# A new order of all units in a hand-scheduled attention and maxout FFN kernel

## The chip, the core and the metric

The kernel runs on one core of one Trainium2 chip. The metric is the device time of one execution in microseconds. Every engine of the core (PE for matmuls and transposes, DVE, ACT and POOL for elementwise work, SP for the DMA queue) takes its own instructions in the order in which the program gives them, and waits for the others by semaphores.

## What is computed

For 4 batches of 768 tokens with 8 heads of 64, attention with a window of 96 tokens back and 8 global tokens, and a distance bias per head; then an FFN whose hidden layer is the largest of three projections:

```python
scores = scale * np.matmul(q, k.transpose(0, 1, 3, 2))
keep = is_global | is_local            # first 8 tokens, or 0 <= row - col < 96
scores = np.where(keep, scores - slopes * dist, -1e9)
a = softmax(scores)
x = np.matmul(a, v)                    # (B, H, S, D) -> (3072, 512)
h = np.maximum(np.maximum(x @ w1, x @ w2), x @ w3)   # 512 -> 768
out = h @ w_out                                       # 768 -> 512
```

Inputs and output are float32; the matmuls work on bf16 casts.

## The kernel before, in words

The tokens are cut into 24 tiles of 128, T = 0 to 23, six to a batch. With a window of 96 a tile needs only its own keys and those of the tile before it, plus the 8 global keys, which are copied over the first 8 columns of the tile before, out of the window's reach. For the FFN the tiles are gathered in seven chunks of 4, 2, 2, 4, 4, 4, 4 (sizes, L89).

The whole order of work is the string SCHEDULE (L25). It is read from left to right (L475); each word is a unit, a letter with numbers, and each unit appends its instructions to the queues of its engines, the DMAs among them to SP's. A word thus stands ahead of a later one only on the engines that both use. A last number (`how`) often picks the engine: 0 ACT, 1 DVE, 2 POOL (`copies`, L176), 4 a DMA transpose for X and T.

- l, c, x: load, cast and transpose on PE a part of q or k, for tiles 0 to 11 (L151, L178, L226). A part is 512 KB. For tiles 0 to 3 part n.0 is q and n.1 is k, of two tiles and all heads; two of them stand ahead of SCHEDULE (L439, L440).
- L, C.0, X: load, cast and transpose q and k of one tile, for tiles 12 to 23 (L160, L185, L245). X with `how` 4 is a DMA transpose from SP (L250), with 0 to 3 eight PE transposes and one or two copies out of PSUM.
- v, C.1: load and cast v of a tile (L169, L189). V: copy the global rows into the first 8 rows of its v (L218), after A of this tile and before A of the next. G: the same for the keys (L209), after S of this tile and before S of the next.
- S(T,g): scores of four heads and the exp on ACT into P (L268); with `how` 1 the bias goes in by two matmuls first (L275), else M multiplies P by a mask on DVE (L302). B and K make the bias and the mask (L291, L297).
- A(T): P times v on PE, then reciprocal and multiply on DVE into xb (L311). T: transpose xb into the chunk's xT, by four PE transposes (L349) and a copy, or with 4 by a DMA from SP (L340).
- F(c,f,j): first layer, four matmuls of 512 or 256 columns (L361); j = 0 is evicted by ACT, 1 and 2 by a max on DVE (L366 to L370). It needs all T of the chunk. O(c,tt): second layer, six matmuls (L376), eviction, output DMA from SP (L383). E: the last chunk's second layer (L390).
- w, W, o, Q: load and cast the weights (L412 to L430). D: matmuls on zeros (L432).

PSUM sets how far PE may run ahead: psH holds three buffers (F, O, E, some of x and T), psT one (x, X, T), and the scores and A share sp0 and sp1, one each. In SBUF the raw parts have five buffers, the raw v six, four cast v go round.

Of the kernel before, what the change touches and what calls it, by code (L numbers as in the profile page):

```python
# [22 lines left out]


SCHEDULE = """  # L25
    K0 K1 K2 K3 K4 K5 l1.0 l1.1 D0.3 c0.0.2 B0.1 B1.1 B2.1 B3.0 K6 B4.1 B5.1 c0.1.1 c1.0.2 x0.0.4 B6.1
    B7.1 x0.1.4 S0.0.1 v0 l2.0 l2.1 K7 S0.1.1 G0.0 S1.0.1 S1.1.0 x1.0.3 c1.1.2 M0.0 M0.1 M1.0 v1 x1.1.4
    C0.1.2 v2 A0.1 G1.2 S2.0.1 M1.1 c2.0.2 x2.0.1 C1.1.1 S2.1.0 G2.2 S3.0.1 M2.0 M2.1 C2.1.1 T0.1 S3.1.1
    M3.0 M3.1 c2.1.2 v3 A1.0 C3.1.0 w0.0 V1.2 x2.1.2 w1.0 A2.1 V2.2 A3.0 T1.0 T2.1 T3.1 W1.0.1 W0.0.0
    G3.2 S4.0.0 S4.1.0 F0.0.0 F0.1.0 M4.0 F0.2.0 F0.3.0 G4.1 S5.0.0 M4.1 S5.1.0 w0.1 W0.1.1 w0.2 W0.2.2  # L30
    V3.2 F0.0.1 F0.1.1 F0.0.2 F0.1.2 v4 C4.1.0 A4.0 V4.2 w1.1 W1.1.2 W2.0.0 F0.4.0 F0.5.0 M5.0 M5.1 w1.2
    W1.2.2 v5 W2.1.0 T4.0 F0.2.1 F0.3.1 l3.0 l3.2 F0.4.1 l3.1 c3.0.2 c3.2.2 F0.5.1 o2 C5.1.0 A5.1 l3.3
    F0.2.2 Q2.2 F0.3.2 W2.2.0 o0 T5.0 F0.4.2 o1 F0.5.2 x3.0.0 F1.0.0 F1.1.0 c3.1.1 F1.2.0 x3.2.0 Q0.2
    F1.0.1 F1.1.1 F1.2.1 l4.0 l4.1 c3.3.0 F1.0.2 F1.1.2 F1.2.2 x3.1.2 x3.3.1 F1.3.0 F1.4.0 Q1.2 F1.3.1
    S6.0.0 S6.1.0 v6 v7 v8 G6.0 F1.3.2 F1.5.0 v9 c4.0.1 F1.4.1 S7.0.0 S7.1.0 G7.2 v10 M6.0 M6.1 M7.0
    M7.1 O0.0.0 F1.4.2 c4.1.1 C6.1.2 C7.1.2 L12 F1.5.1 S8.0.0 S8.1.0 x4.0.0 O0.1.0 A6.0 x4.1.2 A7.1 V7.2
    F1.5.2 v11 T6.0 O0.2.0 T7.1 G8.2 C8.1.2 S9.0.0 S9.1.0 G9.1 v12 v13 O0.3.0 F2.0.0 F2.1.0 S10.0.0 M8.0
    M8.1 M9.0 M9.1 S10.1.0 C9.1.2 L13 L14 F2.0.1 F2.1.1 F2.0.2 A8.0 C12.0.1 F2.1.2 G10.2 O1.0.0 V8.2
    A9.1 X12.1 M10.0 M10.1 C10.1.0 C11.1.0 F2.2.0 S11.0.0 S11.1.0 M11.0 M11.1 L15 F2.3.0 F2.4.0 O1.1.0
    V9.2 A10.1 F2.2.1 V10.2 T8.0 F2.3.1 F2.5.0 T9.0 A11.1 F2.4.1 T10.0 F2.2.2 F2.3.2 T11.1 F2.4.2  # L40
    S12.0.0 S12.1.0 F2.5.1 C13.0.2 C14.0.2 C15.0.1 X13.4 F3.0.0 F3.1.0 F3.0.1 G12.1 C12.1.0 F3.2.0
    F3.1.1 F3.2.1 S13.0.0 S13.1.0 F2.5.2 v14 C13.1.0 C14.1.2 M12.0 M12.1 F3.0.2 F3.1.2 X14.4 F3.2.2
    X15.4 G13.2 M13.0 M13.1 S14.0.0 S14.1.0 F3.3.0 F3.4.0 F3.5.0 M14.0 M14.1 G14.1 A12.0 A13.1 F3.3.1
    F3.4.1 F3.5.1 S15.0.0 M15.0 S15.1.0 G15.0 v15 V13.2 L16 L17 v16 T12.4 v17 M15.1 O2.0.0 C15.1.0 A14.0
    V14.2 F3.3.2 F3.4.2 T13.4 F3.5.2 C16.1.0 C16.0.2 X16.3 T14.4 C17.0.2 A15.1 X17.4 O2.1.0 S16.0.0
    S16.1.0 G16.1 L18 V15.2 L19 T15.1 M16.0 O3.0.0 M16.1 F4.0.0 F4.1.0 F4.0.1 F4.1.1 C18.0.2 L20 C19.0.2
    A16.1 F4.2.0 F4.3.0 S17.0.0 S17.1.0 F4.2.1 F4.0.2 F4.3.1 v18 M17.0 v19 M17.1 X18.3 X19.4 C20.0.0
    V16.2 F4.1.2 C17.1.2 O3.1.1 A17.1 F4.2.2 F4.3.2 S18.0.0 M18.0 S18.1.0 M18.1 F4.4.0 T16.4 T17.4
    F4.4.1 C18.1.2 C19.1.1 F4.4.2 X20.4 G18.1 S19.0.0 S19.1.0 F4.5.0 L21 M19.0 M19.1 v20 F4.5.1 A18.0
    T18.4 F4.5.2 A19.1 T19.4 V19.1 C21.0.1 X21.4 G19.1 L22 C22.0.2 L23 X22.4 O3.2.1 O3.3.0 O4.0.1  # L50
    S20.0.0 S20.1.0 M20.0 G20.0 O4.1.0 F5.0.0 F5.1.0 F5.2.0 S21.0.0 S21.1.0 G21.2 F5.0.1 F5.1.1 M20.1
    M21.0 F5.3.0 F5.0.2 F5.1.2 F5.2.1 F5.2.2 v21 C20.1.1 C21.1.2 F5.4.0 S22.0.0 M21.1 S22.1.0 C23.0.0
    F5.3.1 M22.0 M22.1 F5.5.0 F5.3.2 A20.0 V20.2 G22.2 v22 F5.4.1 X23.4 v23 F5.5.1 T20.4 A21.1 V21.1
    T21.4 F5.4.2 F5.5.2 S23.0.0 S23.1.0 M23.0 O4.2.0 M23.1 C22.1.2 A22.0 C23.1.0 O4.3.0 V22.2 T22.4
    A23.1 T23.4 O5.0.1 O5.1.0 O5.2.1 O5.3.0 F6.0.0 F6.1.0 F6.0.1 F6.0.2 F6.2.0 F6.3.0 F6.4.0 F6.1.1
    F6.2.1 F6.1.2 F6.3.1 F6.4.1 F6.2.2 F6.3.2 F6.5.0 F6.4.2 F6.5.1 F6.5.2 E
"""


# [1 line left out]
def kernel(  # L61
# [272 lines left out]

    def u_XT(T, how):
        c, i = where[T]
        if i == 0:
            xT[c] = xT_pool.tile([128, NP, len(chunks[c]) * 128], BF16, name="xT", tag="xT")
        if how == 4:
            nc.sync.dma_start_transpose(out=xT[c][:, :, i * 128:(i + 1) * 128],  # L340
                                        in_=xb[T].rearrange("p h d -> p (h d)"))
            return
        if early(T):
            tp = psH.tile([128, NP, 128], BF16, name="xtp", tag="h")
        else:
            tp = psT.tile([128, NP, 128], BF16, name="xtp", tag="tp")
        x = xb[T].rearrange("p h d -> p (h d)")
        for jp in range(NP):
            nc.tensor.transpose(tp[:, jp], x[:, jp * 128:(jp + 1) * 128], identb)  # L349
# [4 lines left out]

    def u_F1(c, f, j):
        W = len(chunks[c]) * 128
        if f == 0 and j == 0:
            ht[c] = ht_pool.tile([128, NF, W], BF16, name="ht", tag="ht")
        ps = psH.tile([128, W], FP32, name="h", tag="h")
        for dm in range(4):  # L360
            nc.tensor.matmul(ps, w123[f // 2][:, dm, j, (f % 2) * 128:(f % 2) * 128 + 128],  # L361
                             xT[c][:, dm], start=(dm == 0), stop=(dm == 3))
# [147 lines left out]
```

## Time and profile before

| | us |
|---|---|
| median of three runs | 180.07 (179.84 to 180.17) |
| profiled execution, first to last instruction | 178.3 |
| PE busy, of that | 166.9 |
| DVE busy | 118.9 |
| ACT busy | 103.1 |
| POOL busy | 37.5 |
| first F unit's matmul starts | 23.44 |
| last matmul's end, last output landed | 175.0, 177.3 |

The span of the profiled execution is the time between its first and last instruction. Its time as the runs measure it is not given for itself; the median of the runs is 1.77 us above the span. Busy times are of one execution; matmuls overlap, so that a matmul's duration is longer than the step to the next one. A line number names the line of the kernel that made an instruction (h L361 is the first layer's matmul). "Landing" is the end of a DMA, counted from its issue where a duration is meant.

### The profile page before, as it was taken

To read this page: it belongs to the slowest core of one execution; us is meant where nothing else is said; L and a number is where in the kernel's file an instruction comes from. 1 tells how busy PE (TensorE), PEld (TensorE's weight loads), DVE (VectorE), ACT (ScalarE), POOL (GpSimd) and SP (SyncE) were. 2 spreads that over 40 slices of the span, in tenths; PEclk is the share of its full clock that TensorE was granted. 3 is DMA by queue.
4 is the path that set the end of the run, shared out by engine and by line. 5 is a ranking of instruction groups with operands and counts; after the bars stand their busy time and mean duration, and the time that the engine had idled before them with its cause. 6 is when DMAs were issued, how large, how long until landed. Compare 5 with 4: busy or idle time off the path is not lost.

```text
span 178.3 us, 3960 instructions
## 1 busy us (share of the span) xinstructions
PE 166.9 (94%) x1529; PEld 95.8 (54%) x1551; DVE 118.9 (67%) x237; ACT 103.1 (58%) x160; POOL 37.5 (21%) x65
## 2 busy tenths in 40 slices
PE   3599799999999999999999999999999999999992
PEld 0455644558867677845555555545444555444442
DVE  4519875986787689748979447979358896136620
ACT  4867898646689858555744837351772643341122
POOL 4355203543343112310007024100020401000000
PEclk9999999999999999999999999999999999999998
DMA  5999999999998999989544999769889674610006
GB/s 140 292 271 242 357 320 384 320 361 358 251 193 213 229 254 236 174 171 233 94 90 118 159 247 235 157 132 186 173 153 294 136 143 146 224 42 4 0 11 226
DMA packets 83587, 35.52 MB, mean 199 GB/s; under 512 B 66160, under 2 KB 78320, under 8 KB 83568
## 3 DMA queue, kind: packets, MB, share of 16 engines
q1 hardware_dynamic: 83424, 35.20, 82.8%
q8 instruction: 12, 0.20, 0.5%
q10 hardware_dynamic: 144, 0.07, 0.1%
q14 instruction: 7, 0.06, 0.1%
HBM read 25.17 MB, written 6.29 MB: 176 GB/s over the span
## 4 chain that ended last, share of the span: by engine, by line
PE 85%; DMA 8%; SPq 2%; issue 1%; POOL 1%; DVE 1%; ACT 1%; ACTq 0%
PE h L361 53%; PE po L376 17%; PE sp L283 6%; DMA rawv<-in_v_dram 4%; DMA rawp<-in_q_dram 4%; PE op L322 3%; PE op L325 2%; SPq L174 2%; PE tpp L239 2%; PE xtp L349 1%; SPq L158 1%; POOL qkp L183 1%; PE tp L261 1%; DVE xb L332 0%; ACT va L189 0%
## 5 line engine op out<-in xcount | busy, mean ns | idle before, releaser
L361 PE MATMUL h<-xT,w 128*128 128x512 bf16 (+1 forms) x491 | 99.2, 348 | 0.7 <-issue 0.2
L361 PEld LDWEIGHTS <-w 128*128 128x128 bf16 x504 | 46.9, 98 | 40.5 <-DVE w L427 0.3
L288 ACT ACTIVATE P<-sp 128x1024 bf16<-128x1024 f32 (+1 forms) x48 | 43.4, 955 | 20.6 <-PE sp L283 20.4
L368 DVE TENSOR_TENSOR h<-h,h 128x512 bf16<-128x512 bf16 (+1 forms) x42 | 25.3, 610 | 25.7 <-PE h L361 16.5
L366 ACT CAST h<-h 128x512 bf16<-128x512 f32 (+1 forms) x42 | 21.6, 533 | 21.5 <-PE h L361 21.3
L376 PE MATMUL po<-wo,ht 128*128 128x512 bf16 (+2 forms) x147 | 33.1, 362 | 0.5
L370 DVE TENSOR_TENSOR ht<-h,h 128x512 bf16<-128x512 bf16 (+1 forms) x42 | 25.1, 607 | 3.7 <-PE h L361 3.0
L307 DVE TENSOR_TENSOR P<-P,wmask 128x1024 bf16<-128x1024 bf16 x36 | 24.8, 718 | 3.6 <-ACT P L288 3.5
L376 PEld LDWEIGHTS <-ht 128*128 128x128 bf16 x156 | 14.0, 98 | 13.9
L382 ACT COPY ost<-po 128x512 f32<-128x512 f32 (+2 forms) x20 | 11.2, 564 | 17.8 <-PE po L376 17.7
L332 DVE TENSOR_TENSOR xb<-op,rz 128x512 bf16<-128x512 f32 x24 | 16.6, 692 | 0.8
L283 PEld LDWEIGHTS <-qkT 64*128 64x128 bf16 x352 | 10.2, 96 | 10.0 <-issue 8.0
L283 PE MATMUL sp<-qkT 64*128 64x128 bf16 x352 | 15.2, 223 | 0.4 <-DVE xb L332 0.4
L322 PEld LDWEIGHTS <-P 128*128 128x128 bf16 x192 | 12.5, 97 | 2.5 <-ACT P L288 0.2
L221 POOL COPY va<-vaf 8x260 int32<-8x260 int32 x14 | 6.3, 452 | 34.5 <-PE op L325 34.5
L198 POOL CAST qkb<-raw 128x1024 bf16<-128x1024 f32 x7 | 7.2, 1037 | 27.7 <-DMA raw<-in_q_dram 18.9
L322 PE MATMUL op<-va,P 128*128 128x65 bf16 x160 | 12.3, 193 | 0.7 <-ACT va L189 0.6
L239 PE MATMUL tpp<-identb,qkp 128*128 128x128 bf16 x96 | 8.5, 246 | 4.0 <-POOL qkp L183 3.4
L325 PEld LDWEIGHTS <-P 128*128 128x128 bf16 x160 | 10.4, 97 | 2.2 <-issue 0.7
L239 PEld LDWEIGHTS <-qkp 128*128 128x128 bf16 x96 | 7.0, 111 | 5.8 <-POOL qkp L183 4.3
L325 PE MATMUL op<-va,P 128*128 128x65 bf16 x128 | 9.9, 193 | 0.0
L243 ACT COPY qkT<-tpp 128x1024 bf16<-128x1024 bf16 (+1 forms) x9 | 7.9, 874 | 3.4 <-PE tpp L239 3.4
(66 smaller groups left out, 107.5 us busy)
## 6 DMA issues: line engine op xcount, KB each, us to landing
rawv<-in_v_dram SPq DMA_DIRECT2D x24, 256.0 KB, 4.8
out_dram<-ost SPq DMA_DIRECT2D x23, 256.0 KB, 2.3
rawp<-in_q_dram SPq DMA_DIRECT2D x6, 512.0 KB, 7.2
rawp<-in_k_dram SPq DMA_DIRECT2D x6, 512.0 KB, 7.4
...
```

The costliest lines, as they stand in the source:

```text
L239: nc.tensor.transpose(tp[:, e, j - lo], qb["p", n, s][:, e, 2 * j:2 * j + 2].rearrange("i h d -> i (h d)"), identb)
L283: nc.tensor.matmul(sp[:, hh, j2, ds], qT(T - ds, 1)[hsl, jp], qT(T, 0)[hsl, jp], start=not how, stop=True, skip_group_check=True)
L288: nc.scalar.activation(P[:, :, 0:n], sp.rearrange("p a b d n -> p (a b) d n")[:, :, 0:n], AF.Exp, bias=0.0, scale=scale)
L307: nc.vector.tensor_mul(P, P, wmask[:, g, :, 0:2])
L322: nc.tensor.matmul(o, P[:, i, 0], heads(va[T])[:, h], start=True, stop=(t == 0), skip_group_check=True)
L325: nc.tensor.matmul(o, P[:, i, 1], heads(va[T - 1])[:, h], start=False, stop=True, skip_group_check=True)
L332: nc.vector.tensor_tensor(out=x.rearrange("p (g h) d -> p g h d", g=2), in0=o4[:, :, :, 0:64], in1=rz[:, :, :, None].to_broadcast([128, 2, ...
L361: nc.tensor.matmul(ps, w123[f // 2][:, dm, j, (f % 2) * 128:(f % 2) * 128 + 128], xT[c][:, dm], start=(dm == 0), stop=(dm == 3))
L366: nc.scalar.copy(h01, ps)
L368: nc.vector.tensor_max(h01s[c, f], h01s[c, f], ps)
L370: nc.vector.tensor_max(ht[c][:, f], h01s[c, f], ps)
L376: nc.tensor.matmul(po, ht[c][:, f, tt * 128:(tt + 1) * 128], wo[:, f, cols], start=(f == 0), stop=(f == NF - 1))
```

## The change

SCHEDULE is replaced by another string with the same 483 units: each unit of the old one is in the new one once, in another place, and for many with another last number. Two conditions that make a chunk's buffer at its first use no longer ask for the unit with index 0, since another unit can now be first. What differs in the string:

- The loads on SP at the start: before, after the two that stand ahead of SCHEDULE, `l1.0 l1.1 v0 l2.0 l2.1 v1 v2 v3 w0.0 w1.0 w0.1 w0.2 v4 w1.1 w1.2 v5`; after, `v1 l1.0 l1.1 v0 l2.1 v2 l2.0 v3 w0.0 w0.1 w0.2 w1.0 w1.1 v4 l3.3 v5 w1.2`.
- DMA transposes: T 11 before, 15 after (T7, T8, T9, T10 more); X 9 before, 11 after (X16, X18 more).
- S that begin from the bias: six before (both of tile 0, S1.0, S2.0, S3.0, S3.1), four after (S0.0, S1.1, S2.0, S3.1).
- Engines, as counts of units: casts of v on ACT, DVE, POOL 10, 4, 10 before and 1, 12, 11 after; V 0, 2, 14 and 7, 4, 5; copies of T 7 and 6 on ACT and DVE, then 3 and 6; evictions of O 15 and 5, then 13 and 7; rows of the bias 1, 7, 0 and 2, 3, 3; casts of parts (c) 1, 4, 7 and 2, 5, 5.
- The units of later stages stand in another order throughout; O5 stands among the units of F6, where it was ahead of them.

The diff, with the string cut to its start, a stretch of the middle and its end:

```diff
 SCHEDULE = """
-    K0 K1 K2 K3 K4 K5 l1.0 l1.1 D0.3 c0.0.2 B0.1 B1.1 B2.1 B3.0 K6 B4.1 B5.1 c0.1.1 c1.0.2 x0.0.4 B6.1
-    B7.1 x0.1.4 S0.0.1 v0 l2.0 l2.1 K7 S0.1.1 G0.0 S1.0.1 S1.1.0 x1.0.3 c1.1.2 M0.0 M0.1 M1.0 v1 x1.1.4
-    C0.1.2 v2 A0.1 G1.2 S2.0.1 M1.1 c2.0.2 x2.0.1 C1.1.1 S2.1.0 G2.2 S3.0.1 M2.0 M2.1 C2.1.1 T0.1 S3.1.1
-    M3.0 M3.1 c2.1.2 v3 A1.0 C3.1.0 w0.0 V1.2 x2.1.2 w1.0 A2.1 V2.2 A3.0 T1.0 T2.1 T3.1 W1.0.1 W0.0.0
-    G3.2 S4.0.0 S4.1.0 F0.0.0 F0.1.0 M4.0 F0.2.0 F0.3.0 G4.1 S5.0.0 M4.1 S5.1.0 w0.1 W0.1.1 w0.2 W0.2.2
...
-    A23.1 T23.4 O5.0.1 O5.1.0 O5.2.1 O5.3.0 F6.0.0 F6.1.0 F6.0.1 F6.0.2 F6.2.0 F6.3.0 F6.4.0 F6.1.1
-    F6.2.1 F6.1.2 F6.3.1 F6.4.1 F6.2.2 F6.3.2 F6.5.0 F6.4.2 F6.5.1 F6.5.2 E
+    B4.1 B5.0 v1 K5 D0.3 K1 K3 l1.0 l1.1 K0 B2.2 v0 B1.2 B3.1 c0.0.0 B6.0 B0.1 K4 B7.2 C1.1.2 c0.1.1
+    l2.1 K7 x0.0.2 K2 K6 x0.1.4 S1.1.1 v2 S0.0.1 c1.0.1 G0.0 x1.0.3 c1.1.2 S0.1.0 S1.0.0 M0.1 l2.0
+    x1.1.4 C0.1.2 M0.0 v3 A0.1 M1.0 G1.2 c2.1.1 S2.0.1 S2.1.0 C2.1.1 G2.2 M2.0 w0.0 S3.0.0 w0.1
+    c2.0.2 w0.2 M1.1 T0.1 M2.1 M3.0 w1.0 S3.1.1 G3.2 A1.0 C3.1.1 w1.1 M3.1 V1.0 v4 x2.1.2 l3.3 A2.1
+    x2.0.0 V2.2 W0.0.2 v5 A3.0 T1.1 T2.0 T3.1 W0.1.1 S4.1.0 W0.2.1 w1.2 S4.0.0 M4.0 l3.1 l3.2 V3.1
+    l3.0 v6 v7 F0.0.0 G4.2 F0.1.0 W1.0.2 F0.1.1 F0.0.1 W2.0.0 M4.1 F0.1.2 S5.1.0 S5.0.0 F0.0.2 M5.0
+    o1 F0.3.0 C5.1.2 W1.1.0 M5.1 F0.5.0 C4.1.1 F0.2.0 o0 v9 o2 W1.2.2 c3.3.1 l4.1 l4.0 W2.1.0 v8
+    F0.4.0 A4.0 F0.2.1 c3.2.2 V4.0 x3.3.2 F0.4.1 A5.1 W2.2.1 F0.5.1 T4.0 C6.1.2 c3.1.0 F0.3.1 T5.1
...
+    V9.2 M10.1 F2.5.0 v13 M11.1 F2.1.2 X12.0 F2.2.0 A10.1 F2.0.0 T10.4 O1.0.0 M11.0 F2.5.1 C13.0.1
+    X13.4 F2.0.1 v12 X14.4 V10.2 v14 F2.0.2 C11.1.2 L16 A11.0 F2.5.2 F2.3.0 O1.1.0 C16.0.2 C15.0.0
+    T11.1 X15.4 S12.1.0 S12.0.0 G12.0 F2.3.1 L19 F2.3.2 F3.2.0 F2.2.1 M12.0 F2.2.2 S13.0.0 C12.1.1
...
+    T19.4 F4.1.2 O3.1.0 M17.0 V16.0 V19.0 C22.0.3 F4.2.1 F4.4.0 A17.1 F4.4.1 X21.4 v20 F4.2.2 F4.5.2
+    F4.4.2 M20.0 T17.4 S21.0.0 S21.1.0 C20.1.2 X22.4 v23 O4.1.0 A20.0 M21.1 C23.0.2 F5.5.0 M21.0
...
+    M23.1 M23.0 A22.0 F5.3.1 O4.0.0 V22.2 A23.0 F5.1.2 F5.4.0 T23.4 F5.2.1 T22.4 F5.4.1 F5.2.2
+    F5.5.2 F5.4.2 F5.3.2 F6.2.0 F6.2.1 F6.3.0 F6.2.2 F6.1.0 F6.5.0 F6.3.1 F6.5.1 F6.1.1 F6.0.0
+    F6.1.2 F6.0.1 F6.0.2 F6.4.0 O5.2.0 F6.5.2 F6.3.2 F6.4.1 O5.3.0 O5.1.1 F6.4.2 O5.0.0 E
 """
...
     def u_XT(T, how):
         c, i = where[T]
-        if i == 0:
+        if c not in xT:
             xT[c] = xT_pool.tile([128, NP, len(chunks[c]) * 128], BF16, name="xT", tag="xT")
...
     def u_F1(c, f, j):
         W = len(chunks[c]) * 128
-        if f == 0 and j == 0:
+        if c not in ht:
             ht[c] = ht_pool.tile([128, NF, W], BF16, name="ht", tag="ht")
```

More of the change, by code (lines that the diff above doesn't have):

```diff
@@ L31 @@
[L31 to L54, printed above, removed]
-    A23.1 T23.4 O5.0.1 O5.1.0 O5.2.1 O5.3.0 F6.0.0 F6.1.0 F6.0.1 F6.0.2 F6.2.0 F6.3.0 F6.4.0 F6.1.1
@@ new lines @@
+    l3.0 v6 v7 F0.0.0 G4.2 F0.1.0 W1.0.2 F0.1.1 F0.0.1 W2.0.0 M4.1 F0.1.2 S5.1.0 S5.0.0 F0.0.2 M5.0
+    o1 F0.3.0 C5.1.2 W1.1.0 M5.1 F0.5.0 C4.1.1 F0.2.0 o0 v9 o2 W1.2.2 c3.3.1 l4.1 l4.0 W2.1.0 v8
+    F0.4.0 A4.0 F0.2.1 c3.2.2 V4.0 x3.3.2 F0.4.1 A5.1 W2.2.1 F0.5.1 T4.0 C6.1.2 c3.1.0 F0.3.1 T5.1
+    F0.5.2 F0.3.2 F1.1.0 F1.1.1 Q1.2 c3.0.1 x3.1.0 F0.2.2 F1.1.2 x3.2.2 x3.0.1 F1.2.0 L14 F1.0.0
+    F0.4.2 Q2.2 S7.1.0 c4.1.2 c4.0.2 S6.0.0 F1.2.1 v10 Q0.1 F1.4.0 F1.5.0 F1.0.1 S6.1.0 G6.1 M6.0
+    C9.1.2 S7.0.0 F1.4.1 F1.2.2 C7.1.0 G7.1 F1.3.0 M7.0 F1.3.1 M7.1 S8.1.0 C8.1.2 M8.1 S8.0.0 O0.0.1
@@ new lines @@
+    A7.1 V7.1 M6.1 M8.0 T7.4 O0.3.1 G8.0 S9.0.0 S9.1.0 L12 O0.2.1 G9.1 M9.0 L13 C12.0.2 x4.1.0
+    x4.0.2 A8.1 A6.0 M9.1 O0.1.0 V8.0 F1.5.1 C14.0.3 v11 F1.3.2 S10.1.0 S10.0.0 L15 F1.0.2 T6.1
+    C10.1.1 F1.5.2 A9.1 F2.1.0 G10.1 F2.4.0 F1.4.2 T8.4 F2.1.1 M10.0 S11.1.0 S11.0.0 F2.4.1 T9.4
+    V9.2 M10.1 F2.5.0 v13 M11.1 F2.1.2 X12.0 F2.2.0 A10.1 F2.0.0 T10.4 O1.0.0 M11.0 F2.5.1 C13.0.1
+    X13.4 F2.0.1 v12 X14.4 V10.2 v14 F2.0.2 C11.1.2 L16 A11.0 F2.5.2 F2.3.0 O1.1.0 C16.0.2 C15.0.0
+    T11.1 X15.4 S12.1.0 S12.0.0 G12.0 F2.3.1 L19 F2.3.2 F3.2.0 F2.2.1 M12.0 F2.2.2 S13.0.0 C12.1.1
@@ new lines @@
+    S13.1.0 C13.1.1 F3.5.0 F3.4.0 M13.1 G13.1 M12.1 L18 v15 C14.1.1 F3.2.1 F3.4.1 S14.1.0 M13.0
+    C19.0.2 S14.0.0 F2.4.2 F3.0.0 O2.0.1 G14.0 A12.1 X16.4 F3.4.2 F3.1.0 A13.1 M14.0 C18.0.2 F3.0.1
+    V13.1 M14.1 F3.0.2 S15.1.0 v18 X19.4 S15.0.0 T13.4 X18.4 G15.1 G18.2 F3.1.1 v16 L20 O2.1.0 M15.0
+    A14.1 C20.0.2 M15.1 V14.0 T12.4 T14.4 C15.1.1 F3.5.1 S16.0.0 M16.0 L21 S16.1.0 M16.1 L17 X20.4
+    F3.3.0 C16.1.2 v21 F3.3.1 F3.2.2 A15.0 F3.5.2 F3.1.2 v19 F3.3.2 S18.1.0 S19.0.0 O3.0.1 T15.0
+    S19.1.0 S18.0.0 V15.2 M18.1 O3.3.0 C17.0.2 M18.0 O3.2.0 C18.1.1 X17.4 F4.0.0 G19.2 A16.0 F4.5.0
@@ new lines @@
+    F4.1.0 A18.1 F4.3.0 M19.0 M19.1 F4.3.1 S20.0.0 v17 S20.1.0 F4.0.1 F4.5.1 C19.1.2 G16.1 C21.0.1
+    L23 F4.3.2 F4.2.0 A19.1 G20.2 T18.4 F4.0.2 C17.1.1 F4.1.1 T16.4 L22 S17.1.0 S17.0.0 M17.1 M20.1
+    T19.4 F4.1.2 O3.1.0 M17.0 V16.0 V19.0 C22.0.3 F4.2.1 F4.4.0 A17.1 F4.4.1 X21.4 v20 F4.2.2 F4.5.2
+    F4.4.2 M20.0 T17.4 S21.0.0 S21.1.0 C20.1.2 X22.4 v23 O4.1.0 A20.0 M21.1 C23.0.2 F5.5.0 M21.0
+    C23.1.2 F5.1.0 F5.1.1 v22 G21.0 C21.1.1 F5.0.0 V20.0 F5.0.1 X23.4 S22.1.0 S22.0.0 C22.1.1 O4.2.1
@@ L57 @@
+    F5.0.2 M22.1 A21.1 F5.3.0 G22.2 M22.0 F5.5.1 S23.0.0 T20.4 S23.1.0 O4.3.0 T21.4 V21.1 F5.2.0
+    M23.1 M23.0 A22.0 F5.3.1 O4.0.0 V22.2 A23.0 F5.1.2 F5.4.0 T23.4 F5.2.1 T22.4 F5.4.1 F5.2.2
+    F5.5.2 F5.4.2 F5.3.2 F6.2.0 F6.2.1 F6.3.0 F6.2.2 F6.1.0 F6.5.0 F6.3.1 F6.5.1 F6.1.1 F6.0.0
+    F6.1.2 F6.0.1 F6.0.2 F6.4.0 O5.2.0 F6.5.2 F6.3.2 F6.4.1 O5.3.0 O5.1.1 F6.4.2 O5.0.0 E
 """
```

## The prediction, made before the result was known

> **What bounds the kernel now.** I read the busy table of the page first, then the busy time of the engines in stretches, then the chain that ended last in order of time, then what PE waits for.
>
> ```profile
> PE 166.9 (94%) x1529; PEld 95.8 (54%) x1551; DVE 118.9 (67%) x237; ACT 103.1 (58%) x160; POOL 37.5 (21%) x65
> ```
>
> ```profile
> 0.00:23.00 23.00, 16.15 (x197) 10.10 (x199) 14.27 (x41) 16.75 (x27) 9.38 (x23) 1.00 1.07 263
> 23.00:66.00 43.00, 42.68 (x450) 27.98 (x453) 32.19 (x61) 32.02 (x49) 13.42 (x19) 1.00 1.05 289
> 66.00:120.00 54.00, 53.47 (x514) 30.67 (x520) 40.21 (x80) 32.72 (x52) 10.83 (x16) 1.00 0.88 171
> 120.00:151.00 31.00, 30.74 (x260) 15.64 (x265) 22.86 (x43) 14.63 (x22) 3.84 (x7) 1.00 0.79 177
> 151.00:175.00 24.00, 23.84 (x121) 11.43 (x121) 9.34 (x15) 6.72 (x12) 0.00 (x0) 1.00 0.22 75
> ```
>
> The columns of a stretch are its length, then busy us of PE, PEld, DVE, ACT, POOL, the granted clock, the DMA share and GB/s. From 23 to 175 us PE is busy 150.73 of 152.00 us at clock 1.00: there is no bubble left to take. A busy PE could still be a PE with slack inside, so I laid the units of SCHEDULE end to end at their steady steps in the chain (a 512-wide F1 unit 0.8625 us, a 256-wide one 0.4375, O 1.295, an S of both halves 0.55, A 0.50, four transposes 0.22, E 5.18). From F0.0.0 (start 23.44) they sum to 149.36 and end at 172.80; the last matmul ended at 175.05. The difference of 2.25 grows evenly along the 149 us, no unit adds more than 0.31 at once, and the next gives most of that back: it is step size, not waiting. So **two things alone can shorten this kernel**: a start of F0.0.0 before 23.44, or less PE work after it. Everything else can only add waits.
>
> ```profile
> 13.07 7.08 DMA rawv<-in_v_dram
> 20.18 0.63 ACT va L189
> 20.85 0.19 PE op L322
> 21.54 0.22 DVE rz L331
> 21.78 0.70 DVE xb L332
> 22.52 0.40 PE xtp L349 x4
> 22.92 0.55 PE sp L283 x16
> 23.48 0.34 PE h L361
> ```
>
> These lines (start, length) of the chain tell what sets the start: v of tile 3 lands at 20.16, is cast, A3 runs, is normalised, transposed, then F1 of chunk 0 begins.
>
> **Part 1, the loads at the start.** SP issues ten transfers up to v3 in both orders: four q and k parts of tiles 0 to 3, the two of tiles 4 and 5, v0 to v3. Only the order in between is new (v1 third, v0 sixth, v2 eighth). They land one after another (a 512 KB part 1.8 us after the one ahead, a v 1.2, v3 2.6), so the tenth lands at 20.16 again: the DMA engines are full here (share 1.07), and a v put earlier pushes a q or k part by 1.2 us. I take 20.16 for v3, between 19.5 and 20.9 (v3's own 2.6 against 1.2 of its like is what could vanish or grow). The cast of v3 moves from ACT (0.62) to DVE (0.42), so A3 can start some 0.2 earlier. A2's normalisation (0.24 + 0.61) now stands behind that cast on DVE, then come A3's (0.85), two xT copies (0.34 and 0.42). From 20.2 that is 20.55, 21.4, 22.3, 22.65, 23.1: **F0.0.0 at 23.2**, 0.2 earlier.
> ACT is the other chain: a q cast moves to it (1.05), a bias row more (0.43), x0.0 is copied whole by it (0.92 for 0.57). With 0.67, 0.60, 0.77 and 0.81 us idle in the old order these 1.8 us mostly fit, and the last of the eight exps ends near 19.9 (19.55 before). If it doesn't fit, F0.0.0 slips by up to 0.8. Three bias rows move to POOL, where none is shown: between 0.3 (a 128x128 select) and 0.7 (a 128x512 cast) each; I take 0.5. POOL's first cast is no longer that of q, so they cost nothing until v1 lands near 7.9.
>
> **Part 2, transposes moved from PE to DMA.** T7, T8, T9, T10 (four each) and X16, X18 (eight each) leave PE: 32 transposes. T15.1 to T15.0, X12.1 to X12.0 and the like change the copying engine alone.
>
> ```profile
> 66.08 0.45 PE tp L261 x8
> ```
> ```profile
> L349 PE MATMUL xtp<-identb,xb x52: 219/219/230, 17.2 to 98.9; 128*128 128x128 bf16 x52
> ```
>
> The second line gives 219 ns as one instruction's duration (min, median, max); the first gives the chain 0.45 for eight, 0.055 each. What counts is the step, since they overlap: 32 x 0.055 = **1.76 us less** on PE. All lie after F0.0.0 in PE's full stretch, so all are worth their length.
> [...]
> On the other side stand six transposing DMAs more.
>
> ```profile
> L250 SPq DMA_TRANSPOSE qkT<-qkb x9: 1237/1259/2319, 71.9 to 140.6; - x9
> DMA to landing us min/median/max: 3.1/3.2/4.5
> ```
>
> Each holds SP's queue 1.26 us (an xT one 1.22) and lands after 3.1 to 4.5 (xT 2.4 to 3.4). 4 x 1.22 + 2 x 1.26 = 7.4 us of SP time, beside PE. It costs nothing where the tile is needed later than it lands: T7 is sent some 9 us of PE work before F2.1.0 reads it, X16 and X18 some 8 and 9 before S16 and S18, T22 and T23 (already DMA) 4.3 and 5.2 before F6.2.0. The thin places are X13 (6.6 us of PE work between C13's place and S13; 0.7 for the cast, 4.5 at most to land, and O1.0.0's output ahead of it) and X21 (SP holds it until O3.1.0 is written out, 0.7 after that unit ends; S21 comes 5.7 after the end; 0.4 for the output's issue, 3.1 to 4.5 to land).
>
> **Part 3, casts and copies on other engines.** By the letters of SCHEDULE: v casts ACT 10 to 1, DVE 4 to 12, POOL 10 to 11; V copies POOL 14 to 5, ACT 0 to 7, DVE 2 to 4; T copies on ACT 7 to 3; O evictions DVE 5 to 7. With two more masks on DVE (four S instead of six start from the bias; two matmuls less on PE each, before F0.0.0, hidden) DVE gains some 4 us (8 x 0.42 for v alone), ACT loses some 6, POOL 4. None is at its end on the whole; the question is stretches. Between PE's 47 and 63 us DVE has 17.3 us of work by the durations of its rows against 15.9 of PE, and between 86 and 95.5 some 10.0 against 9.1.
>
> ```profile
> 59.16 2.49 DVE L307 TENSOR_TENSOR P<-P,wmask 128x1024 bf16<-128x1024 bf16 x4
> ```
>
> Four masks of 0.72 take 2.49: steps of 0.59, not 0.72. With steps (mask 0.6, max 0.6 and 0.34, a normalisation 0.85) the two stretches are some 15.2 against 15.9 and 9.0 against 9.1: just under. The old order had such a place too (110 to 121, DVE at its steps almost throughout) without a wait of PE.
>
> **Part 4, the weights.** w0.0, w0.1, w0.2 come ahead of w1.0; the four together land by 27.4 in both orders, w1.1 2.66 later. ACT then casts W2.0, makes two exps, evicts, casts W1.1, evicts twice, casts W2.1, evicts F0.4.0: 0.95 + 1.82 + 0.5 + 0.95 + 1.0 + 0.95 + 0.59 = 6.8, so 34.2 us, just when PE comes to F0.4.1 (23.2 + 11.0), which needs that buffer of three. By durations it is 35.0, a wait of 0.8. I take 0.1.
>
> **Part 5, the order at the end.** O5 moves from ahead of F6 in among it. PE's sum is the same and E with its outputs stays: 0.
>
> **The sum.** Start -0.2, PE -1.76, new waits +0.3 (0.1 for the weights, 0.2 for DVE's two stretches; by durations they would be 0.8, 0.9 and 0.5): -1.7. Profiled span 178.3 - 1.7 = 176.6. The median 180.07 lies 1.77 above the span (start and end around it), kept: **178.4 us**.
>
> **Rivals.**
> *The gain is eaten (0.20).* The start slips 0.4 by ACT's chain and the three places wait by durations rather than steps, 1.3 in all: -1.76 + 1.7 = -0.1, 180.0. For it: an order without bubbles has none to lose, and DVE is at its limit twice. Against: rows of both engines show the steps.
> *SP's queue (0.20), slower.* SP issues in order, and what follows an output waits until PE and an eviction have made it. If a transpose or load behind such an output lands after its reader is due, PE stops, its outputs come later, and so does all behind them. It decides from X21 landing in over 4.6 us (5.7 - 0.7 - 0.4; 4.5 is the longest shown), v20 likewise behind it, and X13, v12 behind O1.0.0. Five links at 0.4 to 0.8 each make 3.0: -1.76 + 3.0 = +1.2, 181.3.
> *Transposes at the page's rate (0.02):* the granted time per transpose would be its 219 ns duration: 32 x 0.219 = 7.0 us, 173.2 with the same start and waits. The even drift above speaks against it.
> That the change doesn't do what it says I don't count: the letters say where each goes.
>
> **How the numbers follow.** Forecast 0.58, with its own range 177.5 to 179.6. A measurement of this kernel can tell some 0.2%, 0.36 us, from no change: 179.71 to 180.43. The eaten gain splits 0.03, 0.12, 0.05; the queue is slower; the page's rate faster: 0.63 faster, 0.12 same, 0.25 slower. The range leaves out the page's rate, the quick end of the start and the worst of the queue: 177.4 to 181.6.
>
> **What would show it.** F0.0.0 near 23.2; weight loads of transposes 32 fewer; PE busy within 1 us of each long stretch after it. Wrong if PE waits for DVE between 50 and 64 or at O3.0, for ACT at F0.4.1, or for a DMA at S13, S21 or A20; or if v3 lands beyond 21.

## The result, and the profile after

The changed kernel takes 184.26 us (median of four runs, 183.83 to 185.28) against 180.07 before: 1.0243 times as long, with a 95% interval of 1.0211 to 1.0276. Forecast were 178.4, between 177.4 and 181.6. Line numbers of the changed kernel are one higher than those of the kernel before: the first layer's matmul is L362 here, the scores are L284, the second layer L377.

The busy table of the page, first line, after:

```profile
PE 166.9 (92%) x1515; PEld 93.6 (51%) x1515; DVE 125.7 (69%) x246; ACT 98.9 (54%) x153; POOL 39.3 (22%) x58
```

PE is as busy as before in a span of 182.1 us instead of 178.3. The stretches of the prediction, after (columns as there: length, PE, PEld, DVE, ACT, POOL, clock, DMA share, GB/s):

```profile
0.00:23.00 23.00, 15.56 (x199) 9.82 (x201) 15.16 (x39) 18.24 (x29) 12.06 (x24) 1.00 1.07 260
23.00:66.00 43.00, 42.22 (x454) 27.15 (x449) 37.59 (x73) 30.60 (x45) 13.56 (x15) 1.00 1.05 288
66.00:120.00 54.00, 50.89 (x485) 28.35 (x483) 39.59 (x79) 28.14 (x44) 9.66 (x13) 1.00 1.22 215
120.00:151.00 31.00, 30.27 (x249) 15.11 (x247) 21.92 (x40) 14.36 (x23) 4.07 (x6) 1.00 0.73 145
151.00:175.00 24.00, 24.00 (x113) 10.84 (x111) 11.14 (x17) 5.26 (x9) 0.00 (x0) 1.00 0.09 33
```

The third row is the one to read. PE lost 3.11 of 54 us there, where before it lost 0.53, and the DMA share rose from 0.88 to 1.22. Within it, from 80 to 95 us, first before and then after:

```profile
80.00:95.00 15.00, 14.84 (x143) 7.86 (x145) 12.74 (x25) 9.48 (x14) 2.04 (x4) 1.00 0.68 131
```
```profile
80.00:95.00 15.00, 13.19 (x137) 7.00 (x135) 12.96 (x27) 6.38 (x11) 3.58 (x3) 1.00 1.33 219
```

DVE has the same work in both, ACT less, POOL 1.5 us more; what is new above all is DMA at 1.33 where the share was 0.68. (Which part of that is the order's and which the transposes' is seen below, at six_on_pe.) The three longest of PE's waits between 23 and 175 us, after (us in total, times, longest); before there is none on another engine or a DMA:

```profile
PE sp L284 <- DMA qkT<-qkb: 2.2, 3, 1.8
PE sp L284 <- POOL qkT L217: 1.0, 1, 1.0
PE h L362 <- DVE h L369: 0.7, 1, 0.7
```

**First wait, S16, 1.81 us at 92.7.** Its X16 is one of the added DMA transposes. SP's timeline has it issued here, in the second line (start, length, then what was issued and the tiles that it writes and reads):

```profile
87.30 1.09 SPq L384 DMA_DIRECT2D out_dram<-ost  x1
88.48 1.42 SPq L251 DMA_TRANSPOSE qkT<-qkb  x1
```

It landed at 94.45, 5.97 after its issue, and PE's scores began at 94.50. SP had issued without a break from 75.2 to 88.4, so X16's slack was the 4.2 us from 88.48 to PE's arrival at 92.7 and not the 8 us of PE work between the words. With the 3.2 us that such a landing took in the median before, it would have landed at 91.7, in time.

**Second wait, S20, 0.96 at 111.7.** The releaser is G19 on POOL, a copy of a few columns. POOL's timeline says why it was late:

```profile
110.63 1.35 POOL L199 CAST qkb<-raw 128x1024 bf16<-128x1024 f32 x1 [5.91 <-DMA raw<-in_k_dram]
111.94 0.66 POOL L217 COPY qkT<-kg 128x32 bf16<-128x32 bf16 x1
```

The cast is C17; it stood ahead of G19 in POOL's queue and waited 5.91 us for the load L17, which landed at 110.5.

**Third wait, a unit of F4, 0.73 at 124.8.** The same on DVE, with its half of the cast C22 behind the load L22 and the max behind that:

```profile
124.48 0.43 DVE L196 CAST qkb<-raw 128x512 bf16<-128x512 f32 x1 [1.56 <-DMA raw<-in_q_dram]
124.82 0.68 DVE L369 TENSOR_TENSOR h<-h,h 128x512 bf16<-128x512 bf16 x1
```

So one late transpose and two late loads. The two waits that the view puts down to DVE and POOL are waits for the stream of DMAs as well. The q and k transposes' row, after (issue time min, median, max in ns; then the landing):

```profile
L251 SPq DMA_TRANSPOSE qkT<-qkb x11: 1253/1415/2366, 72.4 to 132.0; - x11
...
DMA to landing us min/median/max: 3.2/4.4/6.0
```

Before it was 1259 and 3.2 in the median. Units laid end to end as in the prediction give the books: F0.0.0 at 23.37 (-0.07), PE work 147.60 (-1.76), growth over it up to the last matmul's end 7.96 where it was 2.22 (+5.74; the prediction has 2.25, from an end of 175.05 for 175.02), the stretch behind the last matmul 0.14 shorter: +3.77, as the span grew. Gaps of PE of over 0.12 us after F0.0.0 make 4.56 of the 5.74: the three above, 0.33 at 38.1, 0.39 at 56.8 and two of 0.17, at 76.7 (S13, for X13) and at 111.2 (S20, for X20). The rest is in smaller pieces. Of the 4.19 us between the medians 0.42 lie in runs that took longer than the profiled span accounts for.

### The profile page after: what moved, and what is told of

Read it like the earlier page. It is cut to its first block, busy times and chain, and to the rows that moved or that the text cites. A ratio compares the mean times of both kernels' runs of the same rounds, so it can differ in the third digit from the quotient of the medians.

```text
span 182.1 us, 3909 instructions
## 1 busy us (share of the span) xinstructions
PE 166.9 (92%) x1515; PEld 93.6 (51%) x1515; DVE 125.7 (69%) x246; ACT 98.9 (54%) x153; POOL 39.3 (22%) x58
## 2 busy tenths in 40 slices
DMA packets 87875, 36.57 MB, mean 201 GB/s; under 512 B 70448, under 2 KB 82608, under 8 KB 87856
## 3 DMA queue, kind: packets, MB, share of 16 engines
q1 hardware_dynamic: 87712, 36.25, 89.5%
## 4 chain that ended last, share of the span: by engine, by line
PE 68%; DMA 11%; DVE 7%; ACT 3%; issue 3%; SPq 3%; POOL 2%; POOLq 0%; DVEq 0%; ACTq 0%
PE h L362 41%; PE po L377 13%; PE sp L284 6%; DMA raw<-in_k_dram 6%; DMA qkT<-qkb 6%; PE tpp L240 3%; PE op L323 2%; SPq L168 2%; DVE xb L333 2%; PE op L326 2%; DVE P L308 1%; PE sp L276 1%; DVE h L369 1%; ACT wmask L301 1%; ACT P L289 1%
## 5 line engine op out<-in xcount | busy, mean ns | idle before, releaser
L362 PE MATMUL h<-xT,w 128*128 128x512 bf16 (+1 forms) x504 | 101.1, 349 | 1.1 <-DVE h L369 0.7
L362 PEld LDWEIGHTS <-w 128*128 128x128 bf16 x504 | 46.6, 98 | 41.5 <-issue 1.2
L377 PE MATMUL po<-wo,ht 128*128 128x512 bf16 (+2 forms) x156 | 34.1, 363 | 0.0
L308 DVE TENSOR_TENSOR P<-P,wmask 128x1024 bf16<-128x1024 bf16 x37 | 27.7, 765 | 3.2 <-ACT P L289 3.1
L377 PEld LDWEIGHTS <-ht 128*128 128x128 bf16 x156 | 14.1, 98 | 14.8
L284 PE MATMUL sp<-qkT 64*128 64x128 bf16 x352 | 15.4, 223 | 3.8 <-DMA qkT<-qkb 2.2
L383 ACT COPY ost<-po 128x512 f32<-128x512 f32 (+2 forms) x18 | 9.9, 558 | 16.2 <-PE po L377 13.9
L284 PEld LDWEIGHTS <-qkT 64*128 64x128 bf16 x352 | 10.3, 96 | 13.4 <-issue 6.3
L199 POOL CAST qkb<-raw 128x1024 bf16<-128x1024 f32 x7 | 8.0, 1149 | 34.7 <-DMA raw<-in_k_dram 28.5
L383 DVE COPY ost<-po 128x512 f32<-128x512 f32 (+1 forms) x8 | 5.1, 637 | 10.5 <-PE po L377 10.5
L244 ACT COPY qkT<-tpp 128x1024 bf16<-128x1024 bf16 (+1 forms) x10 | 9.1, 922 | 1.8 <-PE tpp L240 1.7
```

Source lines behind the costliest of these rows:

```text
L284: nc.tensor.matmul(sp[:, hh, j2, ds], qT(T - ds, 1)[hsl, jp], qT(T, 0)[hsl, jp], start=not how, stop=True, skip_group_check=True)
L308: nc.vector.tensor_mul(P, P, wmask[:, g, :, 0:2])
L377: nc.tensor.matmul(po, ht[c][:, f, tt * 128:(tt + 1) * 128], wo[:, f, cols], start=(f == 0), stop=(f == NF - 1))
```

## The experiments

The theory that the first runs put to the test (S in the expectations): the stream of DMAs, SP's queue in order and the 16 engines behind it, is full from 66 to 128 us, the six added transposes push every load behind them, and PE pays for it wherever something is due. Rivals: each wait is a local slip of the order, which a local repair removes; or the casts and copies on other engines (DVE and POOL at their limits) make the time. The medians are of the kernel named; each ratio is to the kernel before, measured with it.

| kernel | us | ratio, 95% | last matmul's end, profiled |
|---|---|---|---|
| after | 184.26 | 1.0243, 1.0211 to 1.0276 | 178.93 |
| six_on_pe | 182.69 | 1.0145, 1.0128 to 1.0162 | 176.84 |
| x16_ahead | 185.04 | 1.0274, 1.0226 to 1.0322 | 178.91 |
| two_engines | 186.08 | 1.0344, 1.0300 to 1.0388 | 179.76 |
| three_waits | 185.02 | 1.0265, 1.0240 to 1.0291 | 179.39 |
| six_extra | 186.27 | 1.0339, 1.0293 to 1.0386 | 181.22 |
| six_copy | 183.56 | 1.0192, 1.0175 to 1.0209 | 178.69 |
| six_fix | 182.00 | 1.0109, 1.0083 to 1.0135 | 175.63 |
| six_fix2 | 181.96 | 1.0110, 1.0089 to 1.0131 | 176.40 |
| six_w22 | 184.28 | 1.0232, 1.0213 to 1.0251 | 178.86 |
| pair_apart | 187.87 | 1.0433, 1.0406 to 1.0460 | 181.41 |
| old_engines | 203.81 | 1.1310, 1.1286 to 1.1333 | 198.45 |
| old_X2 | 180.19 | 0.9996, 0.9987 to 1.0005 | 174.00 |
| old_four | 178.61 | 0.9914, 0.9901 to 0.9928 | 173.71 |
| old_five | 184.01 | 1.0206, 1.0184 to 1.0227 | 177.66 |

### six_on_pe: the six tiles transposed on PE again

```diff
-T7.4 ... T8.4 ... T9.4 ... T10.4 O1.0.0 ... X16.4 ... X18.4 G15.1 G18.2 ... F3.3.2
+T7.1 C14.0.3 ... T8.0 ... T9.0 ... O1.0.0 T10.0 ... X16.3 ... G15.1 ... X18.3 G18.2 F3.3.2
```

> The changed order with its six added transposes (T7 to T10, X16, X18) back on PE, T7 and T10 and X18 a few words later so that PE doesn't stand before its input. Theory S (the DMA stream): six transposes fewer shorten the full stream, X16's wait of 1.81 us at S16 is gone, L17 and L22 land earlier and the waits at S20 (1.1) and at F4 (0.7) shrink; PE does 1.76 more. So about 184.3 - 3.0 + 1.8 = 183, and the landing of L17 (110.5 in the changed kernel) comes at least 4 us earlier. Theory O (the order of the loads alone): L17 lands within 2 us of before, the waits at S20 and F4 stay, only S16's goes: 184.3 - 1.8 + 1.8 = 184.3. Theory D (DVE has too much): all waits stay about as they are, 186.

The time came as expected and the three long waits are gone, with 32 transposes more on PE. L17 landed at 107.8, 2.7 us earlier: less than the 4 that I expected. A wait of 0.70 at 66.8 is this kernel's own (X12 waits for a PSUM buffer that T9's copy on ACT still holds). Its row from 80 to 95 us, columns as above:

```profile
80.00:95.00 15.00, 14.89 (x150) 8.11 (x151) 13.06 (x26) 8.41 (x14) 3.14 (x3) 1.00 1.26 212
```

The DMA share is 1.26 (and 1.07 from 66 to 120) without one transpose added, so most of the rise from 0.68 to 1.33 is the new order of the loads; and PE works for 14.89 of the 15 us. So a full stream was no wait in itself. With six transfers more in it (six_extra, below) PE works for 12.99 of the 16 us from 112 to 128, and here for 15.84.

### x16_ahead, two_engines, three_waits: the waits one by one

x16_ahead puts X16 ahead of L18, v15 and an output on SP; two_engines takes G19 to ACT and the cast C22 whole off DVE; three_waits does both.

```diff
-M13.1 G13.1 M12.1 L18 v15 ... X16.4        C17.0.2 ... G19.2 ... C22.0.3
+M13.1 G13.1 M12.1 X16.4 L18 v15 ...        C17.0.2 ... G19.0 ... C22.0.2
```

> The changed order with the word X16.4 moved ahead of L18 and v15 (behind L19) on SP's queue; nothing else. Theories S and O: X16 lands some 5 us earlier, the wait of 1.81 at S16 is gone; L18, v15 and what follows land 1 to 2 us later. By S, where the stream is full, part of the gain is given back at S20 and F4: 182.5 to 183.5. By O 182.4. Theory D: 184.3.

> The changed order with G19 on ACT in place of POOL, and the cast of C22 whole on POOL in place of half on DVE. The theory of casts that wait for a late load ahead of short work on their engine: the waits at S20 (1.1) and F4 (0.7) are gone, 184.3 - 1.8 = 182.5, with S16's wait as before. If these two waits are DVE's load or the transposes themselves: 184.3, and the waits stay.

> Both edits together: X16 ahead of L18, G19 on ACT, C22 whole on POOL; the six transposes stay DMAs. If the three waits are all that the order loses beyond the start: 184.3 - 1.8 - 1.8 = 180.7, with 0.9 us of small waits left. If the stream is too full for six more transposes whatever the order, a new wait comes up behind them and it stays above 182.

In x16_ahead X16 landed at 88.2 and S16 no longer waits for it, yet PE stops at the same spot for 1.11 us, now for a normalisation on DVE, which has a copy of keys (0.92), a max and a mask ahead of it, and goes on at 93.90 instead of 94.50. A wait of 0.51 for an xT transpose follows at 105.3, and S20's and F4's stay, 0.96 each. L17, and the half of L22 that F4 waits for, landed when they had (110.2 and 124.4, for 110.5 and 124.4), so the 0.6 gained at S16 was waited off again at these places: the last matmul's end is that of the changed kernel, 178.91 for 178.93. In two_engines the waits of S20 and F4 are gone, S16's stays at 1.79, and a new one of 1.95 stands at 126.8, for X21's transpose. PE's two longest groups of waits in three_waits, with both repairs:

```profile
PE sp L284 <- DMA qkT<-qkb: 2.3, 3, 1.4
PE sp L284 <- DVE xb L333: 1.1, 1, 1.1
```

The waits that were named are gone and others stand at 76.4, 93.6 and 126.9 (0.70, 1.13, 1.40: 3.2 us for the 3.5 before the repairs). None of the three beats the changed kernel, where a local repair was to bring 182.4, 182.5 and 180.7; theory S had the gain of x16_ahead too high as well (182.5 to 183.5). The local theory falls. Where the loads landed late, PE's gain at one wait (0.6 us at S16 in x16_ahead) was lost at the next.

### six_extra and six_copy: what a transpose costs the stream

Both are six_on_pe with six more DMAs into scratch buffers that nobody reads, at the words where the six transposes had stood (they also read their source tiles, as those did): transposes in six_extra, plain copies of the same tiles in six_copy. PE's work is six_on_pe's.

```diff
+    def u_Y(T):   # a word Y at each place of T7.4, T8.4, T9.4, T10.4, X16.4, X18.4
+        nc.sync.dma_start_transpose(out=scratch, in_=xb[T] or qb[T])   # six_extra
+        nc.sync.dma_start(out=scratch, in_=xb[T] or qb[T])             # six_copy
```

> The kernel with the six transposes on PE, and where each DMA transpose stood, one that writes a scratch tile that nobody reads. Its work on PE is that of the kernel before. Theory S (each transposing DMA takes 1.3 to 1.7 us of a full stream, SP's queue and the DMA engines together): L17 lands 2.5 us or more later than the 107.8 of the kernel without them, L22 2 us later than 118.7, the waits at S20 or F4 come back: 184 to 185.5 against 182.7. If the transposes cost the stream only their bytes (1.05 MB, some 3.6 us at 290 GB/s) or nothing: L17 within 1 us and 182.7 to 183.

> As six_extra (the six tiles transposed on PE, and six more DMAs that nobody reads at the words where the six transposes stood), but the six more are plain copies of the same tiles into the same scratch buffers, the same bytes without transposing. Theory B (a DMA transpose costs the stream its bytes and its issue): L17 lands within 1 us of six_extra's 112.7, L22 within 1 of its 123.8, the waits at S20 and F4 come back, and the time is within 0.5 us of six_extra's 186.27. Theory H (transposing itself costs: at each transpose the trace of the changed kernel shows a hole in the stream, such as 91.0 to 92.2 us, where 34 GB/s moved at engines shown busy): L17 lands below 110.5, L22 below 121.5, at most one of the two waits is left, and the time is below 184.8.

| | six_on_pe | six_copy | six_extra |
|---|---|---|---|
| L17 landed | 107.8 | 110.1 | 112.7 |
| L23 landed | 118.7 | 121.4 | 123.8 |
| L22 landed, the load after it | 122.8 | 125.2 | 127.8 |
| DMA, MB and packets | 35.52, 83587 | 36.57, 84451 | 36.57, 87875 |
| wait of S20, of F4 | none | none, 0.95 | 1.35, 1.19 |
| us | 182.69 | 183.56 | 186.27 |

The expectations give the landings of L23 as those of L22: in the changed order L23 stands ahead of L22 on SP. Landings are those of the second half of a load, k.

PE's two long waits in six_extra (its own line numbers, ten higher):

```profile
PE sp L294 <- DMA qkT<-qkb: 1.4, 1, 1.4
PE h L372 <- DVE h L379: 1.2, 1, 1.2
```

They stand at S20 (now directly for its own transpose, X20) and at F4, as in the changed kernel, brought back by DMAs whose results nobody uses: the stream makes them. Six transposes pushed L17 by 4.9 us, 0.8 each. Half of it, 2.3, is paid by plain copies of the same bytes too, the other half, 2.6 or 0.43 each, by transposing, so theory H of the two held, by all its numbers (121.4 is L23's landing; L22's own moved by 2.4 and 5.0, the same halves). At 186.27 six_extra cost more than the 184 to 185.5 that theory S gave. Which of a transpose's properties costs it wasn't told apart: the six moved their tiles in packets of some 245 bytes (4288 packets for 1.05 MB, where the copies took 864), and in the changed kernel the issue of a transpose held SP for 1.22 us (L341) and 1.42 us (L251) in the median, that of a load of q or k for 0.65 and 1.04 (L168).

### six_fix and six_fix2: what is left without the six transposes

six_fix takes six_on_pe's own wait away; six_fix2 moves an eviction off DVE's queue ahead of A6 as well.

```diff
-V9.2 M10.1 F2.5.0 v13 M11.1 F2.1.2 X12.0 F2.2.0 A10.1      M8.1 S8.0.0 ... O0.2.1
+V9.2 M10.1 F2.5.0 v13 M11.1 F2.1.2 F2.2.0 A10.1 X12.0      M8.1 S8.0.0 ... O0.2.0   (six_fix2)
```

> The kernel with the six transposes on PE, with X12 moved two words later (behind A10), because T9's copy held the one psT buffer and PE waited 0.7 us for it there: a wait that my own edit had made. What the rest of the new order and the moved casts cost beside the kernel before: 182.7 - 0.7 = 182.0, of which the wait at 38 us (0.3 to 0.5), the one near 55 (0.4) and a tail 0.8 longer are known.

> six_fix with the eviction of O0.2 on ACT, which waits there for PE from 51.9 to 53.6, in place of DVE, where it stood ahead of A6's normalisation. Theory D (the one wait of six_fix after 22 us, 0.59 at 53.5, is DVE's queue and nothing hides behind it): the wait goes, the last matmul ends 0.5 to 0.6 earlier than 175.63, so at the 175.0 of the kernel before, and the time is 181.3 to 181.6; what is then left over 180.07 lies behind the last matmul. Theory N (the next thing is late instead): another wait of at least 0.3 comes up between 53 and 70, and the last matmul stays above 175.4.

six_fix is at 1.0109 with one wait of PE on another engine of over 0.2 us after 22 us, 0.60 at 53.5, for A6's normalisation; ahead of that on DVE two masks took 2.54 us beside POOL's casts (50.1). Its profiled execution is 1.4 us longer than the one before: 0.6 by the last matmul, 0.8 behind it, where the last outputs land late. In six_fix2 that wait is gone and this stands for it, at 56.2:

```profile
PE op L323 <- POOL va L190: 0.9, 1, 0.9
```

The time is the same, and theory N held: between 53 and 57 us the queues of DVE and POOL are both late, and a repair of the one shows the other. POOL's two casts of v took 2.89 us here (54.2), beside masks on DVE, where one alone takes 0.62. The last outputs landed in 1.9 us, as before, and not in 2.6, and from the last matmul to the end of the span it takes 3.6 us instead of 4.1 (3.3 before): more than half of six_fix's 0.8 there isn't the order's. So order and engines of the change cost 1.1% without any transpose added, and the six transposes made that 2.4%, where they were to take 1.76 us off.

### six_w22 and pair_apart: the casts of the weights

six_w22 is six_on_pe with W2.2's cast on ACT and T10 moved; pair_apart is six_fix with W1.2's cast on ACT in place of POOL.

```diff
-W1.2.2 ... W2.2.1 ... O1.0.0 T10.0 ... F3.2.0
+W1.2.2 ... W2.2.0 ... O1.0.0 ... T10.0 F3.2.0      (six_w22)
-W1.2.2
+W1.2.0                                             (pair_apart)
```

> The kernel with the six transposes on PE, with the cast of W2.2 on ACT in place of DVE, and T10 a little later. In the changed order that cast took DVE 1.37 us (0.69 elsewhere) beside POOL's cast of W1.2 from the same landing, and PE waited 0.3 to 0.5 for it at 38 us. If that pairing of DVE and POOL is the cause: the wait is gone and the rows of W2.2 are 1.05 on ACT, 0.3 to 1 us faster than 182.7. If DVE was late for its own work: 182.7, and PE waits there again.

> As the kernel with X12 later, with W1.2 cast by ACT in place of POOL, so that DVE's cast of W2.2 (same landing, 36.8 us) has no POOL cast beside it. If a POOL cast holds up a DVE cast: W2.2's row falls from 1.4 - 1.5 to 0.7 and PE's wait at 38 is gone, 0.3 to 0.5 us faster. If DVE's cast is long for another reason: 1.4 again.

six_w22 settles nothing: the moved T10 made a wait of 1.44 at 76.9, and the one at 38 (0.51) stayed, now for ACT's queue. pair_apart is slower by far, for a reason that I hadn't seen: ACT's cast waits for w1.2, which lands at 36.9, with F0.4.0's eviction behind it, and PE waits 4.88 us at 34.6. What it was made for it does show. The cast of W2.2 on DVE, first in the changed kernel, then POOL there, then DVE in pair_apart without a cast on POOL beside it:

```profile
37.04 1.37 DVE L428 CAST w<-wst 128x1024 bf16<-128x1024 f32 x1
```
```profile
36.82 1.04 POOL L428 CAST w<-wst 128x1024 bf16<-128x1024 f32 x1 [2.13 <-DMA wst<-in_moe_w_dram]
```
```profile
43.11 0.71 DVE L428 CAST w<-wst 128x1024 bf16<-128x1024 f32 x1
```

The one beside POOL took nearly twice as long and ended 0.55 us after POOL's, at 38.41. With its 0.71 alone it would have ended at 37.75, before PE came to it at 38.14: that is the wait of 0.33.

### old_engines: the order before on the engines after

75 units of c, C, V, G, W, Q and O of the kernel before get the engine that they have in the changed one; the order stays.

```diff
-c0.0.2 ... c0.1.1 ... W1.0.1 W0.0.0 ... V1.2 ...
+c0.0.0 ... c0.1.1 ... W1.0.2 W0.0.2 ... V1.0 ...   (75 such units)
```

> The order of the kernel before, with each cast, copy and eviction on the engine that the changed kernel gives it (75 units: c, C, V, G, W, Q, O); transposes and their copies as before. Theory D (casts on DVE are the cause): 183 or more, with PE waiting for DVE. Theory S: the engines are a small part, 180.5 to 182, by waits where the old order had no room for them, and no wait for a DMA over 0.5.

The time is in theory D's "183 or more", but far beyond what either theory meant. PE waits 17 us, 9.6 of them for DVE, 3.7 each for POOL and ACT, and none directly for a DMA. The two longest groups:

```profile
PE op L324 <- DVE va L191: 4.5, 3, 1.8
PE sp L285 <- POOL qkT L218: 3.7, 2, 2.2
```

The order wasn't made for these engines, so the run doesn't price the moves in their own order; it shows that the 75 together can't be had in the old one. In the changed kernel a cast that waited 5.91 us for its load (C17) held up the short work behind it on POOL (G19); whether PE's waits for such short work here (3.7 us for copies of keys, L218) came about so was not shown.

### old_X2, old_four, old_five: transposes in the order before

old_X2 sends X16 and X18 by DMA in the order before, where the stream there has room (16 transposes fewer on PE); old_four T8 and T9 as well (24); old_five X12 too (32), with L15 moved behind X14 and its cast ahead of X15.

```diff
-V8.2 A9.1 X12.1 ... T8.0 ... T9.0        v15 V13.2 L16 L17 v16 T12.4 ... C16.0.2 X16.3   L20 ... X18.3 X19.4
+V8.2 A9.1 T8.4 T9.4 X12.1 ...            v15 L16 L17 v16 C16.0.2 X16.4 V13.2 T12.4 ...   L20 X18.4 ... X19.4
```

The first column of the diff is in old_four and old_five alone.

> The order of the kernel before, with X16 and X18 alone as DMA transposes, placed where SP stood idle (X16 ahead of T12, its cast ahead of V13; X18 behind L20). PE does 16 transposes less, 0.88 us. Theory S says that a DMA transpose is free where the stream has room: X16 lands by 91 and S16 doesn't wait; X18 lands by 112 with S18 at 113: 179.2, or 180.1 if X18 is late by one queue's length. If DMA transposes cost more than they save wherever they stand: over 180.4.

> As the kernel with X16 and X18, and T8 and T9 as DMA transposes too, ahead of L15: PE does 24 transposes less, 1.32 us. Theory S: L15, X13 and X14 land some 2.5 us later than in the kernel before (75.6 and 77.8 for the first two X), still ahead of S13 (80) and S14 (83.5): 178.8. If the stream is full there already, S13 or S14 waits 1 us or more: over 179.5.

> The old order with X16, X18, T8, T9 by DMA (178.61) and X12 too, with L15 and its cast moved behind X14. PE does 8 transposes less, 0.44. If the stream still has room between 68 and 80 us: 178.2. If not, S12 or S13 waits for its transpose: over 178.6.

Before, the last matmul ended at 175.02. old_X2 has it at 174.00: 1.02 earlier, 0.88 expected; X16 landed at 89.5 and X18 at 110.7, both in time, and no wait came up. Its time is that of before, as the last outputs took 2.6 us to land instead of 1.8; an instruction fetch of 8 KB lies among them at 175.43, which I didn't test as the cause. old_four's last matmul ends 1.31 earlier, and 24 x 0.055 is 1.32; X13 and X14 landed 2.5 and 2.8 us later, as expected, and no S waited. It takes 178.61 us, less than both kernels. Its page's busy table and the stretch from 66 to 120:

```profile
PE 165.0 (93%) x1506; PEld 94.0 (53%) x1527; DVE 119.0 (67%) x235; ACT 101.0 (57%) x156; POOL 37.9 (21%) x65
```
```profile
66.00:120.00 54.00, 53.37 (x511) 30.16 (x517) 41.53 (x81) 30.49 (x48) 11.32 (x16) 1.00 1.02 190
```

PE is as full as before (53.37 of 54) and the DMA share went from 0.88 to 1.02, not to 1.22. old_five goes one step too far, though not by filling the stream: from 80 to 95 us the DMA share is 0.57, and neither S12 nor S13 waited. L15, moved back, landed at 81.8; its cast stood behind other work on DVE, and SP stood before X15 until the cast was done, with L16 behind it:

```profile
77.44 0.62 SPq L169 DMA_DIRECT2D raw<-in_k_dram  x1
85.60 1.26 SPq L252 DMA_TRANSPOSE qkT<-qkb  x1
```
```profile
84.89 0.69 DVE L200 CAST qkb<-raw 128x1024 bf16<-128x1024 f32 x1
```

So L16 landed at 94.0 (84.3 before), its cast C16 on POOL stood ahead of V13, and PE stopped for V13:

```profile
PE op L327 <- POOL va L223: 2.7, 1, 2.7
```

It is the pattern of the changed kernel's S20, in the order before: a cast behind a late load, short work behind the cast. Here SP's queue, held by a transpose that waited for its input, made the load late, and not a full stream; whether the stream had room for a 25th to 32nd transpose this run doesn't tell.

## Why the prediction was wrong, point by point

- **What bounds the kernel.** Right: two things can shorten this kernel, everything else can only add waits. The one kernel that was faster, old_four, has less PE work and no new wait. The change added waits.
- **Part 1, the start.** F0.0.0 at 23.37 where 23.2 was forecast, near by luck, for two errors worked against each other. v3 landed at 18.85, earlier than the bound of 19.5; but DVE came to its cast only at 20.0, because two masks, the second beside a cast on POOL, took 2.12 us. The chain after, in order of time:

```profile
17.81 1.42 DVE P L308
19.23 0.13 DVE rz L332
19.38 0.69 DVE xb L333
20.07 0.55 DVE va L190
```

  A bias row on POOL took 1.33 us and not 0.3 to 0.7 (nearest rows of other shapes misled me); it cost nothing, for the reason given.
- **Part 2, PE's share.** Right: weight loads of transposes went from 76 to 44 (L349 52 to 36, L261 24 to 8), 32 fewer, at 0.055 us each. old_four shows it as time.
- **Part 2, the stream's share: the step that failed.** "It costs nothing where the tile is needed later than it lands" was worked out with landing times of the order before, and slack was counted in PE work between words. The rows had the warning (share 0.88 and 1.05), and I never summed what the stream would carry. The loads' new order filled it from 80 to 95 us by itself (1.26 in six_on_pe), and the six transposes came on top: a landing of 3.2 became 4.4 in the median and 6.0 at most, SP came to X16's word 4.2 us ahead of its reader and not 8, and the loads behind were late for their casts. In the sum new waits stood at +0.3 and were +5.7. By the medians the six transposes cost 4.0 us (184.26 - 182.00 of six_fix, and the 1.76 that they were to save), order and engines the other 1.9. six_extra shows the mechanism without any other change, +3.6 us over six_on_pe.
- **Part 3, the engines.** 0.2 was forecast for two stretches of DVE. The first, 47 to 63, cost 0.39 in the changed kernel, 0.60 in six_fix and 0.91 in six_fix2 (there for POOL): the place right, the size nearer to the 0.9 by durations that I had put aside. In the second, 86 to 95.5, X16 came last, but DVE was late as well: it ended the normalisation that S16's second half needs too at 93.27, 0.6 after PE had come, and x16_ahead, without X16's wait, stops there for DVE. DVE's longer times beside POOL (W2.2's cast 1.37 us for 0.71, pair_apart) were not in the sum.
- **Part 4, the weights.** F0.4.1 didn't wait for ACT. W2.2's cast on DVE cost 0.33 at 38.1, for the 0.1 that I took, at another word.
- **Part 5, the end.** Right: from the last matmul to the end of the span 3.1 us, 3.3 before.
- **The rivals.** SP's queue was the right one in kind, with wrong places and a price too small: X13 came 0.17 late for S13, X21 only struck in two_engines and three_waits, and X16, listed among the safe ones, struck most; +3.8 of span and not +1.2. I priced it as outputs that hold SP back. What ran was a full stream, in which a late load reaches PE through a cast that stands ahead of other work. Of the signs of being wrong that the prediction named, two came, PE's waits for DVE at 56.8 and for a DMA at S13; there was none at O3.0, F0.4.1, S21 and A20, where it looked for the others.
- **Left open.** The 1.1% of order and engines without the transposes: the late queues between 53 and 57 us are 0.6 to 0.9 us of its 1.9, by two kernels; the rest is spread between runs and behind the last matmul, and wasn't traced to a unit. The rows of both show DVE and POOL beside each other (masks of 2.54, casts of 2.89); that parting them would bring the 0.6 to 0.9 back was not tried.
